# Bringing transposed activations through VectorE and DRAM instead of TensorE, in a fused attention and mixer block

## The chip, the cores and the metric

The kernel runs on one core of a Trainium2 chip. The metric is device time in microseconds (us), the median of several executions. Profiles are taken on one execution each; "span" is the time from its first to its last instruction, and the execution's own time is a little longer.

In the text TensorE, VectorE, ScalarE, GpSimd and SyncE are also called PE, DVE, ACT, POOL and SP, as in the profile. SP issues all DMAs of this kernel, in program order.

## The reference

With S = 2048 tokens of D = 576 features, all float32:

```python
x = A_x                       # (1, 2048, 576)
xn = _layernorm(x)
return x + _A_ref(xn, wqkv, wo) + _B_ref(xn, w1, w2, w3, w4)

# A: 32 heads of 18; token s attends to s, s-2, ..., s-14 (8 places); softmax; o @ wo
# B:
h  = gelu(layernorm(x) @ w1)                  # h in 4 channel groups
hs = concat(h[group g] shifted by +1,-1,+2,-2 tokens) @ w2
x1 = x + hs
return x1 + gelu(layernorm(x1) @ w3) @ w4     # hidden width 4608
```

Here the "x" of B is xn, the normalised input. Three tensors have to be turned from "token on a partition" to "feature on a partition" before a matmul can contract over features, besides xn itself: z = layernorm(xn), the layernorm of x1, and the attention output o.

## The kernel before

Tokens are handled in 16 tiles of 128 (index t), and in 4 blocks of 512 (index b). Y holds the running sum, token on partition, for all 16 tiles. Matmuls work on float32 split in two parts: a "hi" part rounded to fp32r and a "lo" part, the rest. A transposed block of 512 tokens is a tile of nine slices `[128, 9, 512]`: slices 0 to 3 the hi part of features 0 to 511, slice 4 the last 64 features (hi on partitions 0 to 63, lo on 64 to 127), slices 5 to 8 the lo part. A contraction over 576 features is 14 matmuls (the list PAIRS), whose first two read slice 0 and whose third reads slice 5.

Every engine executes its instructions in the order in which the program emits them (the schedule is manual); what looks concurrent is written out by hand, by placing each step at some iteration of a loop of matmuls. The stages:

1. **qkv.** For each tile t the x tile is loaded, normalised into Y, transposed (`prep_x`), and multiplied by wqkv in two halves (`q_half`); the result goes to DRAM (`qkvd`). Transposed blocks live in `ring`, a pool of two buffers, asked for with `ring_block(key)`.
2. **mix.** For each block b: four `mix_tile` and one `mix_rem`, in the order tiles 0, 1, 2, the remainder, tile 3. They multiply z by w1 (14 matmuls of 512 columns, or 9), and ScalarE applies gelu twice as it evicts PSUM, once to the hi part and once to float32; VectorE subtracts for lo. `mix_rem` also moves rows between partitions with eight small DMAs (v from u) and leaves five later steps in the list `todo`. w2 is loaded and split in this stage.
3. **W2 loop.** For each tile t: 28 matmuls of 288 columns (`mm_tok`), the result added to Y by VectorE, and the statistics of x1 (`stats`). Later the first weights of the MLP are split here too.
4. **MLP.** 72 units (c, b), c over pairs of 128 hidden channels, b over the token blocks. A unit runs two `up` (14 matmuls of 512 columns, two gelus, a subtraction) and the four `down` of the unit before (12 matmuls of 288 columns each, added to Y by VectorE). From the fourth unit on, `bg` interleaves pieces of the attention, which runs on VectorE from `qkvd`, head group by head group, and writes its output to `od` in DRAM; it ends before unit NU-4. The list LATE names the tiles of x1 that are normalised and transposed inside the first units; those of blocks 0 and 1 are handled within the W2 loop.
5. **Wo loop.** For each tile: o @ wo, with the load of o and of x, the sum and the store of the output.

PSUM has two buffers `psa` (tag a: mix_tile, mix_rem, up) and three `psb` (tag b: everything else). The transposition in use is `transposes`: four TensorE transposes of 128x128 per tile, one more for two tiles' tails of 64 features, then ScalarE copies PSUM to the hi slices and VectorE subtracts for the lo slices:

```python
for k in range(4):
    pe.transpose(p0[:, k, :], src[:, k * 128:(k + 1) * 128], ident)
if tail:
    pe.transpose(p1[:rows], tail[0], ident)
act.copy(xt[:, 0:4, c], p0)
dve.tensor_tensor(xt[:, 5:9, c], p0, xt[:, 0:4, c].bitcast(F32), op=ALU.subtract)
```

It is called by `prep_x` (x), `z_prep` (z, in the last four tiles of the qkv stage and in mix), `n_prep` (x1, tiles 6 to 13 of the W2 loop and units 0 to 5) and `prep_o` (o, in the final downs and the Wo loop). `z_norm` and `n_norm` write the normalised tile just ahead of it.

Of the kernel before, what the change touches and what calls it, by code (L numbers as in the profile page):

```python
# [45 lines left out]
def fused_block(ctx, tc, x, wqkv, wo, w1, w2, w3, w4, out):  # L46
# [19 lines left out]
    BN = base.tile([128, 4, 2, 6], F32, name="bn")  # L66
    qkvd = dram.tile([24, HALO + S, GC], F32, name="qkvd")
# [4 lines left out]
    def tail_half(t):  # L72
        if t % 2 == 0:
            ztail[t // 2] = base.tile([128, 128], F32, name="ztail", bufs=2)
        return ztail[t // 2][:, t % 2 * 64:t % 2 * 64 + 64]

    def norm_z(dst, kind, t):
        norm(dst, Y[:, t, :512], kind, t)
        norm(tail_half(t), Y[:, t, 512:], kind, t)
# [36 lines left out]

    def split_w(dst_hi, dst_lo, raw):
        act.copy(dst_hi, raw)  # L118
        dve.tensor_tensor(dst_lo, raw, dst_hi.bitcast(F32), op=ALU.subtract)
# [20 lines left out]
    zp = {}  # L140

    def z_norm(t):
        zp[t] = w1pool.tile([128, 512], F32, name="z", bufs=2)
        norm_z(zp[t], 1, t)

    def z_prep(t):
        xt = ring_block(("z", t // 4))
        transposes(zp[t], pair_tail(ztail[t // 2], xt, t), xt, (t % 4) * 128)
# [176 lines left out]
    load_w1(1)  # L325
    for t in range(4, NT):
        for h in range(2):
            q_half(t, h)
            if h == 0:
# [11 lines left out]
            else:  # L341
                if t == NT - 4:
                    z_norm(0)
                    z_norm(1)
                if NT - 3 <= t < NT - 1:
                    z_prep(2 * (t - NT + 3))
                    z_norm(2 * (t - NT + 3) + 2)
# [13 lines left out]
    pool.memset(T4[:, S:S + 4].bitcast(F32), 0.0)  # L361

    def load_w2(k):
        r = mpool.tile([128, D], F32, name="rz", tag="rz", bufs=2)
# [11 lines left out]
    def mix_tile(b, m):  # L376
# [5 lines left out]
        g32 = mpool.tile([128, 512], F32, name="g32", bufs=1)  # L382
        c = 2 + b * 512
        hi = H[0][m][:, c:c + 512]
        act.activation(hi, ps, AF.Gelu_apprx_tanh)
        act.activation(g32, ps, AF.Gelu_apprx_tanh)
# [4 lines left out]
    def mix_rem(b):  # L391
# [4 lines left out]
        u = mpool.tile([128, 512], F32, name="u", bufs=2)  # L396
        v = mpool.tile([128, 512], F32, name="v", bufs=2)
        act.copy(u, ps)
# [23 lines left out]
    for b in range(NB):  # L422
        for i, m in enumerate((0, 1, 2, 4, 3)):
            nz = 4 * (b + 1) + i
# [44 lines left out]
    def n_norm(t, zpool):  # L469
        zp[t] = zpool.tile([128, D], F32, name="rz", tag="rz", bufs=2)[:, :512]  # L470
        norm_z(zp[t], 2, t)

    def n_prep(t):
        xt = x1n.get(t // 4)
        if xt is None:
            xt = x1n[t // 4] = ring_block(("n", t // 4))
        transposes(zp[t], pair_tail(ztail[t // 2], xt, t), xt, (t % 4) * 128)
# [3 lines left out]
    for t in range(NT):  # L481
        ps = psb.tile([128, 2, 512], F32, name="ps", tag="b")
        if 6 <= t < 14:
            n_norm(t - 6, mpool)
# [17 lines left out]
        if 6 <= t < 14:  # L502
            n_prep(t - 6)
        if 2 <= t and todo:
            todo.pop(0)()
    mp.__exit__(None, None, None)
# [5 lines left out]
    hp = ctx.enter_context(tc.tile_pool(name="hp", bufs=2, reuse_waits="tile"))  # L512

# [98 lines left out]
    def up(c, b, i):  # L612
# [7 lines left out]
        act.activation(hi, ps, AF.Gelu_apprx_tanh)  # L620
        act.activation(g32, ps, AF.Gelu_apprx_tanh)  # L621
# [23 lines left out]
    LATE = {(0, 0): (8, 9), (0, 1): (10, 11), (1, 0): (12,), (1, 1): (13,), (2, 0): (14,), (2, 1): (15,)}  # L645
    Wo = None
    oT = {}
# [25 lines left out]
    otile, xagain = {}, {}  # L673

    def load_o(t):
        if t % 2 == 0 and t < NT:
            src = od[t * 128:(t + 2) * 128, :].rearrange("(a p) d -> p a d", a=2)
            otile[t // 2] = opool.tile([128, 2, 512], F32, name="ot", bufs=2)
            sp.dma_start(otile[t // 2], src[:, :, :512])
            ztail[t // 2] = base.tile([128, 128], F32, name="ztail", bufs=2)  # L680
            sp.dma_start(ztail[t // 2].rearrange("p (a c) -> p a c", a=2), src[:, :, 512:])
# [6 lines left out]
    def prep_o(t):  # L688
        if t >= NT:
            return  # L690
        oT[t] = opool.tile([128, 9, 128], F32R, name="oT", bufs=3)
        o = otile[t // 2]
        tail = (ztail[t // 2], [(oT[t - 1], 0), (oT[t], 0)]) if t % 2 else None
        transposes(o[:, t % 2, :], tail, oT[t], 0)
        dve.tensor_tensor(Y[:, t, :], Y[:, t, :], xagain[t], op=ALU.add)

    for u, (c, b) in enumerate(units):
# [5 lines left out]
        if u == NU - 4:  # L703
            while not state["done"]:
                bg(1e9)
            open_wo()
            load_wo(0)
            load_wo(2)
        if u == NU - 3:
            split_wo(0)  # L710
            load_wo(4)
            load_o(0)
            load_o(2)
# [6 lines left out]
        for i in range(C):  # L720
            bg(r, False)
            ts = LATE.get((u, i), ())
            for t in ts:
                n_norm(t, hp)
            up(c, b, i)
            for t in ts:
                n_prep(t)
# [68 lines left out]
```

## Time and profile before

| | |
|---|---|
| median of 3 runs | 1323.08 us (1322.8 to 1323.17) |
| profiled execution | 1322.94 us, span 1321.2 us |
| TensorE matmuls busy | 1312.1 us (99%) |
| VectorE busy | 921.9 us (70%) |
| ScalarE busy | 348.2 us (26%) |
| GpSimd busy | 35.2 us (3%) |
| DMA | 93.76 MB, mean 71 GB/s |

A row of a group reads: line, engine, operation, output <- inputs, shapes, count, then busy us, mean ns of one, and the idle time of the engine just before, with what ended it. "L102" is line 102 of the kernel before. Matmuls are pipelined, so the duration of one is longer than the distance to the next: what a piece of TensorE's stream costs is read from start to start. A row of the timeline gives start us, us, engine, line and operation, with equal neighbours merged. A row of the table by window gives the window, its length, each engine's busy time, the granted TensorE clock (1.00 is full), the busy share of the DMA engines and GB/s.

### The profile page before, as it was taken

How to read it: one execution, taken by the hardware profiler on the slowest of the kernel's cores; microseconds unless marked ns; L12 is line 12 of the kernel's file. 1: busy time of each engine (PE TensorE's matmuls, PEld its weight loads, DVE VectorE, ACT ScalarE, POOL GpSimd, SP SyncE). 2: the span in 40 equal slices, each digit the busy share in tenths (PEclk: the TensorE clock that was granted, in tenths of full speed). 3: DMA queues.
4: the chain of work that ended last, by engine and by line, in shares of the span. 5: the costliest groups of instructions: out<-in, count | busy, mean ns of one | idle time of the engine just before them, and what ended most of it. 6: DMA issues, size and time to landing. Idle time of an engine off the chain costs nothing.

```text
span 1321.2 us, 18855 instructions
## 1 busy us (share of the span) xinstructions
PE 1312.1 (99%) x7894; PEld 1208.0 (91%) x7894; DVE 921.9 (70%) x1332; ACT 348.2 (26%) x633; POOL 35.2 (3%) x92
## 2 busy tenths in 40 slices
PE   8999999999999999999999999999999999999998
PEld 8999998899899999999999999999999999999998
DVE  6443326687676778878868868878877886884454
ACT  4322225411423222222122222223213223122111
POOL 2010100011000000000000000000000000000000
PEclk9999999999999999999999999999999999999999
DMA  7644322020112021221221220220320200212164
GB/s 211 152 107 108 98 68 69 18 82 28 59 30 80 20 71 39 71 71 39 71 71 29 80 71 20 90 71 20 90 71 19 82 28 20 71 42 95 46 192 140
DMA packets 120325, 93.76 MB, mean 71 GB/s; under 512 B 73504, under 2 KB 100000, under 8 KB 120240
## 3 DMA queue, kind: packets, MB, share of 16 engines
q1 hardware_dynamic: 120240, 92.56, 23.9%
q8 instruction: 62, 1.02, 0.3%
q14 instruction: 23, 0.19, 0.0%
HBM read 67.83 MB, written 23.66 MB: 69 GB/s over the span
## 4 chain that ended last, share of the span: by engine, by line
PE 96%; DVE 2%; ACT 1%; SPq 1%; issue 1%; DMA 0%; POOL 0%; DVEq 0%; ACTq 0%; POOLq 0%
PE ps L636 34%; PE p L616 34%; PE ps L133 18%; PE ps L230 3%; PE p L380 3%; PE ps L102 2%; PE p L272 0%; PE p L395 0%; PE p L764 0%; DVE bn L88 0%; PE ps L105 0%; ACT xt L107 0%; DVE xt L111 0%; SPq L370 0%; DVE xt L114 0%
## 5 line engine op out<-in xcount | busy, mean ns | idle before, releaser
L636 PE MATMUL ps<-W,hi 128*128 128x288 f32 x2304 | 397.9, 294 | 0.5 <-DVE oT L114 0.5
L636 PEld LDWEIGHTS ps<-W,hi 128*128 128x128 f32 x2304 | 339.5, 188 | 6.1 <-PE ps L102 0.7
L620 ACT ACTIVATE hi<-p 128x512 fp32r<-128x512 f32 x144 | 86.2, 599 | 619.3 <-PE p L616 619.3
L636 PE MATMUL ps<-W,lo 128*128 128x288 f32 x1152 | 245.3, 294 | 0.0
L616 PE MATMUL p<-xt,W 128*128 128x512 f32 x1008 | 235.4, 390 | 0.0
L616 PE MATMUL p<-x1n,W 128*128 128x512 f32 x1008 | 234.9, 389 | 0.0
L622 DVE TENSOR_TENSOR lo<-g,hi 128x512 fp32r<-128x512 f32 x144 | 99.7, 692 | 193.2 <-ACT g L621 193.2
L639 DVE TENSOR_TENSOR Y<-ps,Y 128x576 f32<-128x576 f32 x288 | 212.8, 751 | 16.3 <-PE ps L636 16.1
L616 PEld LDWEIGHTS p<-x1n,W 128*128 128x128 f32 x1008 | 187.2, 188 | 36.8
L616 PEld LDWEIGHTS p<-xt,W 128*128 128x128 f32 x1008 | 187.1, 188 | 36.9
L636 PEld LDWEIGHTS ps<-W,lo 128*128 128x128 f32 x1152 | 185.4, 187 | 0.0
L133 PE MATMUL ps<-WQ,xt 128*128 128x432 f32 x672 | 135.3, 360 | 0.0
L133 PEld LDWEIGHTS ps<-WQ,xt 128*128 128x128 f32 x672 | 125.2, 188 | 5.2
L111 DVE TENSOR_TENSOR xt<-ps,xt 128x512 fp32r<-128x512 f32 x40 | 27.6, 689 | 87.2 <-ACT xt L110 52.1
L568 DVE TENSOR_TENSOR prod<-q,k 128x1152 f32<-128x1152 f32 x64 | 86.5, 1351 | 0.0
L571 DVE TENSOR_REDUCE L<-prod 128x64 f32<-128x1152 f32 x64 | 86.2, 1347 | 0.0
L621 ACT ACTIVATE g<-p 128x512 f32<-128x512 f32 x144 | 85.4, 593 | 0.0
L548 DVE TENSOR_TENSOR prod<-v,L 128x1152 f32<-128x1152 f32 x56 | 75.6, 1350 | 0.0
L552 DVE TENSOR_TENSOR o<-o,prod 128x1152 f32<-128x1152 f32 x56 | 75.6, 1350 | 0.0
L118 ACT CAST W<-rawf 128x640 fp32r<-128x640 f32 x72 | 50.5, 702 | 68.9 <-PE ps L636 62.2
L133 PE MATMUL ps<-Wo,oT 128*128 128x288 f32 x420 | 59.1, 298 | 0.2
L133 PEld LDWEIGHTS ps<-Wo,oT 128*128 128x128 f32 x420 | 56.2, 188 | 1.4 <-issue 1.4
(103 smaller groups left out, 941.9 us busy)
## 6 DMA issues: line engine op xcount, KB each, us to landing
qkvd<-stg SPq DMA_DIRECT2D x24, 432.0 KB, 3.4
rawf<-in_B_w_dram SPq DMA_DIRECT2D x36, 288.0 KB, 3.0
rawf<-in_B_w_dram SPq DMA_DIRECT2D x36, 256.0 KB, 2.9
xin<-in_A_x_dram SPq DMA_DIRECT2D x16, 288.0 KB, 3.8
q<-qkvd SPq DMA_DIRECT2D x8, 576.0 KB, 3.8
k<-qkvd SPq DMA_DIRECT2D x8, 576.0 KB, 5.7
v<-qkvd SPq DMA_DIRECT2D x8, 576.0 KB, 5.9
od<-o SPq DMA_DIRECT2D x8, 576.0 KB, 4.9
```

Source lines behind the costliest of these rows:

```text
L118: act.copy(dst_hi, raw)
L133: pe.matmul(ps[:, h, :n], xs(a), ws(b, h), start=i == 0, stop=i == len(PAIRS) - 1)
L548: dve.tensor_tensor(dst, vv, Lf[:, :, w:w + 1].to_broadcast([128, TPP * GH, HD]), op=ALU.mult)
L552: dve.tensor_tensor(o, o, dst, op=ALU.add)
L568: dve.tensor_tensor(prod.rearrange("p (j h) d -> p j (h d)", h=GH), q, k[:, r0:r0 + TPP, :], op=ALU.mult)
L571: dve.tensor_reduce(Lf[:, :, w], prod, axis=AX.X, op=ALU.add)
L616: pe.matmul(ps, W3[f][:, w, :], x1n[b][:, a, :], start=n == 0, stop=n == len(PAIRS) - 1)
L620: act.activation(hi, ps, AF.Gelu_apprx_tanh)
L621: act.activation(g32, ps, AF.Gelu_apprx_tanh)
L622: dve.tensor_tensor(lo, g32, hi.bitcast(F32), op=ALU.subtract)
L636: pe.matmul(ps[:, k, :HF], h[:, col], w[:, p, k * HF:(k + 1) * HF], start=n == 0, stop=n == len(seq) - 1)
L639: dve.tensor_tensor(yv, ps[:, :, :HF], yv, op=ALU.add)
```

## The change

TensorE no longer transposes z, x1 and o; it still transposes x. In place of that:

- `turn(src, t)`: VectorE transposes the 576 columns of a normalised tile in 32x32 squares, in two instructions, into the staging tile ST `[128, 20, 128]` (the tail twice). A 32x32 transpose stays within its quadrant of 32 partitions, so the feature blocks are still in the wrong partitions.
- `put(key)`: after four tiles, four DMAs write ST, 32 partitions each, to a DRAM buffer `[5, 128, 512]`, so that every feature finds its row. ST is a single buffer.
- `get(key, xt)`: one DMA reads the buffer back into slices 4 to 8 of the transposed block.
- `split_x(xt)`: for the whole block, three ScalarE copies make the hi slices and two VectorE subtractions the lo slices.

The columns of a block then stand in the order (quadrant, tile, token) and not (tile, quadrant, token). For z and x1, ScalarE puts them in order as it evicts (`in_order` reads PSUM permuted, `by_token` writes in token order). For o the load is permuted instead: `load_o` reads a block of o in four DMAs, one per quadrant.

The steps are placed anew. z: turns in tiles 7, 8, 10, 11, 13 and 14 of the qkv stage and in mix block 0; the read of block b+1 at the start of mix block b and its split after the third mix step. x1: turns of blocks 0 and 1 in tiles 4 to 7 and 9 to 12 of the W2 loop, reads in tiles 9 and 14, splits in tiles 11 and 15; block 2 in the two ups of unit 0, block 3 in unit 1; their reads and splits in units 1 and 2, between the ups. o: turns with the downs of the last three units and in tiles 0 to 3 of the Wo loop, reads and splits one unit later, for block 3 in tiles 5 and 7. The five steps that `mix_rem` leaves are all done by tile 3 of the W2 loop.

```diff
+    def turn(src, t):
+        c = slice(32 * t, 32 * t + 32)
+        dve.transpose(ST[:, 4:20, c], src[:, :512].rearrange("p (j c) -> p j c", c=32))
+        dve.transpose(ST[:, 0:4, c].rearrange("p (a j) c -> p a j c", a=2),
+                      src[:, 512:].rearrange("p (j c) -> p j c", c=32)[:, None, :, :]
+                      .to_broadcast([128, 2, 2, 32]))
+
+    def put(key):
+        xd[key] = dram.tile([5, 128, 512], F32, name="xd", bufs=4)
+        for q in range(4):
+            sp.dma_start(dram_ap(xd[key], 128 * q, [[512, 32], [32 * 512, 20], [1, 128]]),
+                         ST[32 * q:32 * q + 32])
+
+    def get(key, xt):
+        sp.dma_start(xt[:, 4:9, :].bitcast(F32), xd[key].rearrange("k p c -> p k c"))
+
+    def split_x(xt):
+        raw = xt.bitcast(F32)
+        act.copy(RT[64:128, :], raw[64:128, 4, :])
+        act.copy(xt[0:64, 4, :], raw[0:64, 4, :])
+        act.copy(xt[:, 0:4, :], raw[:, 5:9, :])
+        dve.tensor_tensor(xt[64:128, 4, :], raw[64:128, 4, :], RT[64:128, :].bitcast(F32),
+                          op=ALU.subtract)
+        dve.tensor_tensor(xt[:, 5:9, :], raw[:, 5:9, :], raw[:, 0:4, :], op=ALU.subtract)
+
+    def in_order(blk):
+        return blk.rearrange("p (q t c) -> p t q c", q=4, t=4)
+    def by_token(blk):
+        return blk.rearrange("p (t q c) -> p t q c", q=4, t=4)
+    def quads(t_, b, q):
+        return dram_ap(t_, (512 * b + 128 * q) * D, [[D, 32], [32 * D, 4], [1, D]])
...
+    ZT = {7: 0, 8: 2, 10: 4, 11: 6, 13: 8, 14: 10}
     for t in range(4, NT):
         for h in range(2):
             q_half(t, h)
...
-                if t >= NT - 2:
-                    z_prep(2 * (t - NT + 2) + 1)
-                    z_norm(2 * (t - NT + 2) + 3)
+                if t == 12:
+                    get(("z", 0), ring_block(("z", 0)))
+            elif t == 13:
+                split_x(xring["z", 0])
+            if t in ZT:
+                z_turn(ZT[t] + h)
+                if h and ZT[t] % 4 == 2:
+                    put(("z", ZT[t] // 4))
+    get(("z", 1), ring_block(("z", 1)))
...
-        act.activation(hi, ps, AF.Gelu_apprx_tanh)
-        act.activation(g32, ps, AF.Gelu_apprx_tanh)
+        act.activation(by_token(hi), in_order(ps), AF.Gelu_apprx_tanh)
+        act.activation(by_token(g32), in_order(ps), AF.Gelu_apprx_tanh)
...
     for b in range(NB):
+        if 0 < b < NB - 1:
+            get(("z", b + 1), ring_block(("z", b + 1)))
         for i, m in enumerate((0, 1, 2, 4, 3)):
...
-            if b + 1 < NB and i < 4:
-                z_prep(nz)
-                if nz + 2 < NT:
-                    z_norm(nz + 2)
+            if b + 1 < NB and i == 2:
+                split_x(xring["z", b + 1])
+            if b == 0 and i > 0:
+                z_turn(12 + i - 1)
+                if i == 4:
+                    put(("z", 3))
...
+    def n_turn(t, zpool):
+        z = zpool.tile([128, D], F32, name="rz", tag="rz")
+        norm(z, Y[:, t, :], 2, t)
+        turn(z, t % 4)
+        if t % 4 == 3:
+            put(("n", t // 4))
...
+        while len(todo) > max(0, 3 - t):
             todo.pop(0)()
...
+        k = {4: 0, 5: 1, 6: 2, 7: 3, 9: 4, 10: 5, 11: 6, 12: 7}.get(t)
+        if k is not None:
+            n_turn(k, rzpool)
+        if t in (9, 14):
+            nb = t // 14
+            x1n[nb] = ring_block(("n", nb))
+            get(("n", nb), x1n[nb])
+        if t in (11, 15):
+            split_x(x1n[t // 15])
...
-    LATE = {(0, 0): (8, 9), (0, 1): (10, 11), (1, 0): (12,), (1, 1): (13,), (2, 0): (14,), (2, 1): (15,)}
+    LATE = {(0, 0): (8, 9), (0, 1): (10, 11), (1, 1): (12,)}
...
+    def load_o(b):
+        if b < NB:
+            otile[b] = opool.tile([128, 4, D], F32, name="ot", bufs=1)
+            for q in range(4):
+                sp.dma_start(otile[b][32 * q:32 * q + 32], quads(od, b, q))
+    def o_turn(b, t):
+        turn(otile[b][:, t, :], t)
+        if t == 3:
+            put(("o", b))
...
             up(c, b, i)
-            for t in ts:
-                n_prep(t)
+            for t in LATE.get((u, i), ()):
+                n_turn(t, tp)
+            if u in (1, 2) and i == 0:
+                get(("n", u + 1), x1n[u + 1])
+            if u in (1, 2) and i == 1:
+                split_x(x1n[u + 1])
+            if u >= NU - 2 and i == 0:
+                get(("o", u - NU + 2), o_block(u - NU + 2))
...
             for j in range(4):
                 bg(r, j == 1)
                 down(*prev, j)
+                if u == 1 and j < 3:
+                    n_turn(13 + j, tp)
+                if u >= NU - 3:
+                    o_turn(u - NU + 3, j)
+                if u >= NU - 2 and j == 1:
+                    split_x(xo[u - NU + 2])
+            if u >= NU - 3:
+                load_o(u - NU + 4)
...
+    get(("o", 2), o_block(2))
     for j in range(4):
         if j < 3:
-            prep_o(j)
+            add_x(j)
             load_xa(j + 2)
         down(*prev, j)
+    split_x(xo[2])
...
     for t in range(NT):
+        if b == 0:
+            o_turn(3, s)
+        if t == 5:
+            get(("o", 3), o_block(3))
+        if t == 7:
+            split_x(xo[3])
```

More of the change, by code (lines that the diff above doesn't have):

```diff
@@ L139, in fused_block, with z_turn @@
     W1R = w1pool.tile([128, 5, 128], F32R, name="W1R")
[L140 to L148, printed above, removed]
+    room(w1pool)
+    def z_turn(t):
+        z = w1pool.tile([128, D], F32, name="z", bufs=1)
+        norm(z, Y[:, t, :], 1, t)
+        turn(z, t % 4)
     qp = tc.tile_pool(name="qp", bufs=1, reuse_waits="tile")
@@ L467, in fused_block @@
     x1n = {}
[L469 to L477, printed above, removed]
+    def n_turn(t, zpool):
+        z = zpool.tile([128, D], F32, name="rz", tag="rz")
+        norm(z, Y[:, t, :], 2, t)
+        turn(z, t % 4)
+        if t % 4 == 3:
+            put(("n", t // 4))
     load_f(0)
@@ L686, in load_xa, with o_block, add_x @@
             sp.dma_start(xagain[t], xf[t * 128:(t + 1) * 128, :])
[L688 to L695, printed above, removed]
+    def o_turn(b, t):
+        turn(otile[b][:, t, :], t)
+        if t == 3:
+            put(("o", b))
+    def o_block(b):
+        if b < 2:
+            xo[b] = ring_block(("o", b))
+        else:
+            xo[b] = xp.tile([128, 9, 512], F32R, name=f"x1n{b}")
+        return xo[b]
+    def add_x(t):
+        if t < NT:
+            dve.tensor_tensor(Y[:, t, :], Y[:, t, :], xagain[t], op=ALU.add)
     for u, (c, b) in enumerate(units):
```

78 lines of the change are left out of this document (34 added, 44 removed).

## The prediction

> **What bounds the kernel now.** I read the page first, then TensorE's instructions in order of time around the three places where z, x1 and o are transposed, then the merged chain of waits, the prices by tile, and the DMA rows.
>
> ```profile
> span 1321.2 us, 18855 instructions
> ...
> PE 1312.1 (99%) x7894; PEld 1208.0 (91%) x7894; DVE 921.9 (70%) x1332; ACT 348.2 (26%) x633; POOL 35.2 (3%) x92
> ...
> PE 96%; DVE 2%; ACT 1%; SPq 1%; issue 1%; DMA 0%; POOL 0%; DVEq 0%; ACTq 0%; POOLq 0%
> ```
>
> TensorE (PE) is the bound: every microsecond off its stream comes off the span, and every wait it is given is added, since there is hardly an idle moment to absorb one. The profiled execution took 1322.94 us, 0.14 us from the median of the runs (1323.08), so I add to and take from 1322.9.
>
> Start times in order, from three windows of TensorE's timeline, and the merged chain:
>
> ```profile
> 172.88 0.60 PE L102 MATMUL ps<-ident,z 128*128 128x128 f32 x4
> 173.23 5.77 PE L133 MATMUL ps<-WQ,xt 128*128 128x432 f32 x28
> ...
> 196.80 3.36 PE L380 MATMUL p<-xt,W 128*128 128x512 f32 x14
> ```
> ```profile
> 245.86 13.01 PE L380 MATMUL p<-xt,W 128*128 128x512 f32 x56 [0.39 <-ACT g L386]
> 258.70 2.20 PE L395 MATMUL p<-xt,W1R 128*128 128x512 f32 x9
> 260.74 3.34 PE L380 MATMUL p<-xt,W 128*128 128x512 f32 x14
> 263.92 3.34 PE L133 MATMUL ps<-W,h 128*128 128x288 f32 x24
> ...
> 267.62 3.35 PE L133 MATMUL ps<-W,h 128*128 128x288 f32 x24
> ```
> ```profile
> 365.36 6.35 PE p L616 x28
> ...
> 1216.44 6.36 PE p L616 x28
> 1229.14 6.36 PE p L616 x28
> ```
> ```profile
> 1314.04 3.87 PE L764 MATMUL p<-Wo,oT 128*128 128x288 f32 x28
> ```
>
> **What is removed.** Undisturbed pieces first. A mix block is four mix_tiles, 258.70 - 245.86 = 12.84, and one mix_rem, 260.74 - 258.70 = 2.04: 14.88. A token tile of the W2 loop (and of the Wo loop, also 28 matmuls of 288 columns) is 267.62 - 263.92 = 3.70. A unit of the MLP is 1229.14 - 1216.44 = 12.70, of which the two ups take 6.35 and the four downs the other 6.35. Against these:
>
> - z: the mix stage ran 263.92 - 196.80 = 67.12; four blocks are 59.52. Saved 7.6, and four tiles in the qkv stage at 173.23 - 172.88 = 0.35 give 1.4 more: 9.0.
> - x1: W2 loop and units 0 to 2 ran 365.36 - 263.92 = 101.44; 16 x 3.70 + 6.35 + 2 x 12.70 = 90.95 (unit 0 has no downs). Saved 10.5.
> - o: from the last unit to the last tile 1314.04 - 1229.14 = 84.90; 12.70 + 6.35 + 15 x 3.70 = 74.55. Saved 10.35.
>
> Together 29.9 us, small stalls included. If all else were hidden the time would be 1293.
>
> **What is added: prices.** Everything else must hide under TensorE. The rows nearest to the new operations:
>
> ```profile
> L119 DVE TENSOR_TENSOR WQ<-raw,WQ x13: 451/758/1509, 7.5 to 45.2; 128x288 fp32r<-128x288 f32 x5, 128x864 fp32r<-128x864 f32 x4, 128x576 fp32r<-128x576 f32 x2, 128x1296 fp32r<-128x1296 f32 x2
> ```
> ```profile
> L118 ACT CAST WQ<-raw x13: 427/680/1278, 6.7 to 44.2; 128x288 fp32r<-128x288 f32 x5, 128x864 fp32r<-128x864 f32 x4, 128x576 fp32r<-128x576 f32 x2, 128x1296 fp32r<-128x1296 f32 x2
> ```
> ```profile
> L94 DVE TENSOR_SCALAR z<-Y,mv,rs x16: 536/542/549, 160.0 to 242.0; 128x512 f32<-128x512 f32 x16
> ```
> ```profile
> 316.41 0.76 DVE L495 TENSOR_TENSOR Y<-ps,Y 128x576 f32<-128x576 f32 x1 [0.19 <-PE ps L133]
> ...
> 318.37 0.68 DVE L111 TENSOR_TENSOR xt<-ps,xt 128x512 fp32r<-128x512 f32 x1
> ```
> ```profile
> L620 ACT ACTIVATE hi<-p 128x512 fp32r<-128x512 f32 x144 | 86.2, 599 | 619.3 <-PE p L616 619.3
> ```
>
> The shortest and longest of L119 (288 and 1296 columns) give VectorE 1.05 ns a column, of L118 ScalarE 0.84. So split_x on 2048 columns is 1.51 + 752 x 0.00105 = 2.3 us on VectorE (plus 0.7 for the 512-column tail) and, on ScalarE, 1.28 + 752 x 0.00084 = 1.9 plus two copies of 0.6: 3.1. ScalarE goes first, so a block is ready 3.1 + 2.3 = 5.4 after its read has landed. No row shows a VectorE transpose. The fastest 512-column row is 0.54, the dearest case twice L119's rate, 1.2; I take 0.6 (one pass over the columns) and 0.27 for the 128-column one. A turn with its norm (about 0.58) is then 1.45 us, without it 0.87; an add of Y with its statistics is 318.37 - 316.41 = 1.96. A gelu that reads in permuted order costs 0.6 by L620; if it doubled, two would take 2.4, still under the 3.18 us of the 14 matmuls behind them, so I cost it at nothing.
>
> The DRAM trip has no row, but its parts do:
>
> ```profile
> 410.00:411.00 1.00, 1.00 (x10) 1.00 (x9) 0.00 (x0) 1.00 (x3) 0.00 (x0) 1.00 1.00 406
> 532.80:533.80 1.00, 1.00 (x6) 0.84 (x5) 0.56 (x1) 0.00 (x0) 0.00 (x0) 1.00 1.00 245
> ```
> ```profile
> q<-qkvd SPq DMA_DIRECT2D x8, 576.0 KB, 3.8
> ...
> od<-o SPq DMA_DIRECT2D x8, 576.0 KB, 4.9
> ```
>
> With every DMA engine busy, 288-byte rows written to DRAM go at 245 GB/s, long rows read at 406. Less its bytes, the od write leaves 4.9 - 0.59/0.245 = 2.5 us of fixed time, the q read 3.8 - 0.59/0.406 = 2.35. put moves 640 x 2 KB = 1.31 MB in 512-byte rows: 5.7 us at 406, 7.8 at 245; I take 7.0, nearer the short-row end. get moves the same in 2 KB rows: 5.5. A trip is 12.5 us (9.5 to 13.5), and 12.5 + 5.4 = 17.9 from the last turn to the block. [...]
>
> **x1, where it is late.** T counts from the start of the W2 loop (263.92). VectorE and ScalarE run in program order, so an early split_x holds all that follows it: the next adds of Y, which free psb, and the gelus, which free psa. Turns 0 to 3 end near T = 34.4 (tile 7's matmuls end at 29.6; the steps left from mix_rem and two weight splits put VectorE a microsecond or two behind). Block 0: put 41.4, read 46.9, ScalarE 50.0, VectorE 52.3; psb covers that. But tile 12's add now starts at 52.3, so turn 7 ends at 55.8. Block 1: put 62.8, read 68.3, ScalarE 71.4, VectorE 73.7. TensorE has done unit 0's ups at 59.2 + 6.35 = 65.6, and the next up needs block 1 and a psa buffer whose gelu stands behind the split: about 73. **7 us lost.**
>
> Block 2: after 73.7 VectorE does two lo and four turns (7.2): 80.9; put 87.9. Ahead of the read on SP stand the five loads of attention (576 KB three times, 504 KB twice: 2.8 MB, 9 us at some 300 GB/s), so read 99.8, ScalarE 102.9, VectorE 105.2, first add 105.9. TensorE ran two ups and the three downs that psb holds, to 84.1. **21.8 lost.** Block 3: three more turns and adds, 111.7; put 118.7, read 124.2, split 129.6, add 130.3; TensorE stands from 118.6: **11.7 lost.** Sum 40.5.
>
> **Mix.** M counts from 196.80. Block 1 is read at M = 7.2, but its split follows the third gelu (10.8): VectorE done 16.2, block due 14.9: 1.2 lost. Block 2's read comes on SP behind the load of W2 row 3, eight v moves, the put of z's block 3 and eight small W2 loads:
>
> ```profile
> 211.97 0.59 SPq L400 DMA_DIRECT2D v<-u  x1
> ...
> 216.40 0.59 SPq L401 DMA_DIRECT2D v<-u  x1
> 217.08 3.76 SPq L370 DMA_DIRECT2D rz<-in_B_w_dram  x8
> ```
>
> VectorE frees W2's buffer after split_x and a turn, M = 18.5 to 19; the v moves take 216.40 + 0.59 - 211.97 = 5.0: 24; the put's four issues 2.4; the small loads 3.8: 30.4. Read 35.9, ScalarE 39.0, VectorE 41.3, while block 2 is due at 16.1 + 14.9 = 31.0: 9.6 lost. Block 3: 0.8. Sum 11.6.
>
> **o.** The read of o for block 0 goes behind load_wo:
>
> ```profile
> 1205.23 0.38 SPq L663 DMA_DIRECT2D rawf<-in_A_wo_dram  x1
> ```
>
> It lands near 1212, and the turns end at 1218.2 with the downs of the third-last unit. From then on a block has this cycle: put 7.0; load_o's data behind the put's, landed at +10; turn, add, turn +12.5; get's data behind both, landed +13.2, split +18.6; two adds and two turns +21.8. A unit is 12.70, so VectorE ends at 1240.0 and 1261.8, the last down at 1264.9 instead of 1229.14 + 12.70 + 6.35 = 1248.2: 16.7 lost. Tile 1 of the Wo loop then waits for an add behind add_x(2), whose xagain load stands on SP behind get(o, 2): 8.3 more. Sum 25. The last block has time: read by about 1301, used at tile 12. The qkv stage has slack for its puts (a tile is two halves of 5.6 us).
>
> **Sum:** 1322.9 - 29.9 + 40.5 + 11.6 + 25.0 = 1370.
>
> **Rivals.**
>
> - All is covered, 1293, faster. It decides at the trip: seven trips lie on the path (three of x1, one of z, three of o), so each microsecond off one is worth 7. The 77 us of stalls sink below 29.9 when a trip is under 12.5 - 47.2/7 = 5.8 us. For: TensorE's stream does lose 29.9. Against: the two fixed times alone are 4.85. Chance 0.06.
> - Short trips: 512-byte rows move as fast as long ones and reads start at once, 9.5 us; 3 x 7 = 21 less: 1349. For: the fixed times come from loaded queues. Chance 0.24.
> - Only x1 is late; in mix and o a buffer or the queue order leaves more room than I found: 1322.9 - 29.9 + 40.5 = 1333.5. Chance 0.08.
> - Restarts run slow. TensorE starts the program slowly:
>
> ```profile
> L272 PE MATMUL p<-ident 128*128 128x128 f32 x24 | 5.4, 423 | 1.4 <-POOL ident masks.py:199 1.4
> ```
>
> These 24 take 5.4 us, later four take 0.35 (172.88 to 173.23), so 24 would take 2.1: 3.3 lost. If each long stall ends so, three are followed by work that sets the end (after z's block 2, x1's block 3, tile 1 of Wo): 10 us, 1380. No row shows it after a stall within the span, and the granted clock reads 1.00 in the windows, so the sum has it at nothing. [...] In the same case I count dearer additions: transposes at 1.2 us put some 0.6 on each of the 15 or so turns that stand on these chains, 9 us, together up to 1390. Chance 0.2.
>
> The forecast itself, 1355 to 1375, has 0.42.
>
> **How the numbers follow.** About 0.2% (2.6 us) is what a measurement can tell here. Only the first rival is faster: 0.06. Same would need stalls of 27 to 32 us, between the first and third: 0.02. Slower 0.92. The range leaves out the first rival, most of the third and the far end of the fourth: 1335 to 1392.
>
> **What would show it.** Right: TensorE's transposes fall from 290 to the 74 of x and its idle time rises from 9 us to some 80, named VectorE, ScalarE or a DMA, in three clusters: one stall near 10 us in mix, three behind the W2 loop of which the middle is the longest, two or three in the last 130 us. A single trip put to get near 12.5. Wrong: TensorE still 99% busy, trips near 6 us, or stalls within u >= 3, where I expect none from permuted gelus.

## The result

The changed kernel took 1412.91 us (median; 1411.92 to 1417.27), the kernel before 1322.97 us beside it: a ratio of 1.0686, interval 1.0664 to 1.0709. It is 89.9 us slower. The prediction said slower, 1370 us, at most 1392; the mechanism came true and the size did not.

The page of the changed kernel, its span, TensorE's row, the granted clock by slices, and the chain by engine:

```profile
span 1411.5 us, 18421 instructions
PE 1305.7 (93%) x7678; PEld 1198.5 (85%) x7678; DVE 942.9 (67%) x1324; ACT 347.6 (25%) x573; POOL 36.8 (3%) x92
PEclk9999998998679999999999999999999999998789
PE 75%; DMA 9%; DVE 6%; SPq 4%; ACT 3%; issue 1%; ACTq 0%; DVEq 0%
```

TensorE fell from 99% to 93% busy: 9 us of idle time became 106. 216 instructions fewer took only 6.4 us off its busy time, because some ran at a lower granted clock (mean 0.963, before 1.000), which the third line shows around slices 7, 11 and 38. On the chain, 22% of the span now belongs to DMAs, VectorE, SP and ScalarE (9, 6, 4 and 3%; 4% before).

TensorE's timeline, the first matmul of each stage and those that end a long stall (in brackets the idle time before, and what ended it):

```profile
194.68 9.70 PE L421 MATMUL p<-xt,W 128*128 128x512 f32 x42
...
240.53 1.22 PE L421 MATMUL p<-xt,W 128*128 128x512 f32 x2 [12.77 <-ACT u L439]
242.37 10.67 PE L421 MATMUL p<-xt,W 128*128 128x512 f32 x40 [0.62 <-DVE xt L146]
...
274.52 1.75 PE L173 MATMUL ps<-W,h 128*128 128x288 f32 x12
...
352.21 9.56 PE L670 MATMUL p<-xt,W 128*128 128x512 f32 x28 [11.19 <-ACT g L675]
387.67 1.33 PE L690 MATMUL ps<-W,hi 128*128 128x288 f32 x4 [21.14 <-DVE Y L693]
413.99 1.33 PE L690 MATMUL ps<-W,hi 128*128 128x288 f32 x4 [11.40 <-DVE Y L693]
417.04 7.60 PE L670 MATMUL p<-x1n,W 128*128 128x512 f32 x28
...
1282.75 6.52 PE L670 MATMUL p<-x1n,W 128*128 128x512 f32 x28
1319.25 1.30 PE L690 MATMUL ps<-W,hi 128*128 128x288 f32 x4 [12.64 <-DVE Y L693]
1350.11 28.16 PE L173 MATMUL ps<-Wo,xt 128*128 128x288 f32 x196 [12.92 <-DVE Y L693]
1404.44 3.87 PE L843 MATMUL p<-Wo,x1n 128*128 128x288 f32 x28
```

The stalls stand in three clusters, as forecast. The differences of these starts, set against those of before, give each stage's share:

| stage | before | after | forecast | measured |
|---|---|---|---|---|
| qkv, to mix | 196.80 | 194.68 | -1.4 | -2.1 |
| mix | 67.12 | 79.84 | +4.0 (-7.6 + 11.6) | +12.7 |
| W2 loop and units 0 to 2 | 101.44 | 142.52 | +30.0 (-10.5 + 40.5) | +41.1 |
| the middle | 863.78 | 865.71 | 0 | +1.9 |
| last unit to last tile | 84.90 | 121.69 | +14.65 (-10.35 + 25) | +36.8 |

The sum of the differences is +90.4. The trips that set these stalls, on SP (start, time on the queue, line; `xd<-st` is put, `xt<-xd` and `x1n<-xd` are get, `ot<-od` is load_o):

```profile
219.77 4.41 SPq L133 DMA_DIRECT2D xd<-st  x4
224.28 6.05 SPq L411 DMA_DIRECT2D rz<-in_B_w_dram  x8
230.43 0.39 SPq L137 DMA_DIRECT2D xt<-xd  x1
...
309.86 4.18 SPq L133 DMA_DIRECT2D xd<-st  x4
318.41 0.38 SPq L137 DMA_DIRECT2D xt<-xd  x1
...
1302.21 4.14 SPq L133 DMA_DIRECT2D xd<-st  x4
1306.46 4.41 SPq L732 DMA_DIRECT2D ot<-od  x4
1311.06 0.38 SPq L137 DMA_DIRECT2D xt<-xd  x1
1328.96 4.14 SPq L133 DMA_DIRECT2D xd<-st  x4
```

and on ScalarE, the first instruction of each split, which waits for the read:

```profile
236.94 0.61 ACT L141 CAST rt<-xt 64x512 fp32r<-64x512 f32 x1 [12.72 <-DMA xt<-xd]
324.54 0.62 ACT L141 CAST rt<-xt 64x512 fp32r<-64x512 f32 x1 [38.27 <-DMA xt<-xd]
1320.61 0.61 ACT L141 CAST rt<-xt 64x512 fp32r<-64x512 f32 x1 [21.18 <-DMA xt<-xd]
```

With nothing beside it a put takes 318.41 - 309.86 = 8.55 us and the read 324.54 - 318.41 = 6.1: a trip of 14.7, where the prediction had 7.0 + 5.5 = 12.5. The puts of blocks 1 and 3 of x1 took 8.4 and 8.6, their reads 6.4 and 6.1. In the o stage the same two take 8.85 and 9.55, since load_o stands between them on SP, with the DMA engines 84% and 89% busy in the two stretches (79% and 67% in those of block 0).

The prices of the added instructions, in groups by line (count, total, mean ns):

```profile
L125 DVE STREAM_TRANSPOSE st<-rz 128x512 f32<-128x512 f32 x16 | 11.4, 712 | 10.0 <-DMA xd<-st 9.5
L126 DVE STREAM_TRANSPOSE st<-rz 128x128 f32<-128x128 f32 x16 | 4.3, 270 | 0.0
L143 ACT CAST xt<-xt 128x2048 fp32r<-128x2048 f32 x8 | 15.2, 1898 | 0.0
L146 DVE TENSOR_TENSOR xt<-xt 128x2048 fp32r<-128x2048 f32 x8 | 18.3, 2293 | 13.0 <-ACT xt L143 13.0
L674 ACT ACTIVATE hi<-p 128x512 fp32r<-128x512 f32 x144 | 86.1, 598 | 605.6 <-PE p L670 605.6
```

These were right or near: 0.71 and 0.27 for a turn (forecast 0.6 and 0.27), 1.9 and 2.3 for the split as forecast, 598 ns for a gelu in permuted order against 599 in plain order.

### The profile page after: what moved, and what is told of

It reads as the page before. It is cut to its first block, busy times and chain, and to the rows that moved or that the text cites. A ratio compares the mean times of both kernels' runs of the same rounds, so it can differ in the third digit from the quotient of the medians.

```text
span 1411.5 us, 18421 instructions
## 1 busy us (share of the span) xinstructions
PE 1305.7 (93%) x7678; PEld 1198.5 (85%) x7678; DVE 942.9 (67%) x1324; ACT 347.6 (25%) x573; POOL 36.8 (3%) x92
## 2 busy tenths in 40 slices
DMA packets 157636, 125.20 MB, mean 89 GB/s; under 512 B 72416, under 2 KB 129632, under 8 KB 157552
## 4 chain that ended last, share of the span: by engine, by line
PE 75%; DMA 9%; DVE 6%; SPq 4%; ACT 3%; issue 1%; ACTq 0%; DVEq 0%
PE p L670 29%; PE ps L690 29%; PE ps L173 12%; DMA xt<-xd 3%; PE ps L267 3%; DMA x1n<-xd 2%; DMA xd<-st 2%; SPq L133 1%; DVE xt L146 1%; DVE st L125 1%; ACT xt L143 1%; PE p L421 1%; SPq L732 1%; DMA xa<-in_A_x_dram 1%; DVE Y L693 1%
## 5 line engine op out<-in xcount | busy, mean ns | idle before, releaser
L690 PE MATMUL ps<-W,hi 128*128 128x288 f32 x2304 | 404.4, 297 | 57.9 <-DVE Y L693 57.9
L690 PEld LDWEIGHTS ps<-W,hi 128*128 128x128 f32 x2304 | 345.1, 191 | 65.5 <-DVE Y L693 47.1
L690 PE MATMUL ps<-W,lo 128*128 128x288 f32 x1152 | 248.4, 297 | 0.0
L670 PE MATMUL p<-xt,W 128*128 128x512 f32 x1008 | 237.6, 392 | 11.3 <-ACT g L675 11.2
L670 PEld LDWEIGHTS p<-xt,W 128*128 128x128 f32 x1008 | 188.8, 189 | 49.8 <-ACT g L675 11.6
L693 DVE TENSOR_TENSOR Y<-ps,Y 128x576 f32<-128x576 f32 x288 | 212.1, 749 | 8.3 <-PE ps L690 8.3
L690 PEld LDWEIGHTS ps<-W,lo 128*128 128x128 f32 x1152 | 188.4, 190 | 0.0
L421 PE MATMUL p<-xt,W 128*128 128x512 f32 x224 | 55.4, 403 | 16.8 <-ACT u L439 13.4
L421 PEld LDWEIGHTS p<-xt,W 128*128 128x128 f32 x224 | 42.6, 193 | 29.0 <-ACT u L439 14.7
L159 DVE TENSOR_TENSOR W<-rawf,W 128x640 fp32r<-128x640 f32 x72 | 56.4, 785 | 0.0
```

Source lines behind the costliest of these rows:

```text
L421: pe.matmul(ps, W1[:, w, m * 128:(m + 1) * 128], xt[:, a, :], start=i == 0, stop=i == len(PAIRS) - 1)
L670: pe.matmul(ps, W3[f][:, w, :], x1n[b][:, a, :], start=n == 0, stop=n == len(PAIRS) - 1)
L690: pe.matmul(ps[:, k, :HF], h[:, col], w[:, p, k * HF:(k + 1) * HF], start=n == 0, stop=n == len(seq) - 1)
L693: dve.tensor_tensor(yv, ps[:, :, :HF], yv, op=ALU.add)
```

## The experiments

The theory (A) was: the block comes late by the length of its trip, VectorE and ScalarE are held by the split in their program order, and each stage pays for itself. Rivals: the parts share one cause (B), the added work costs wherever it stands (D), or another wait takes the place of any that is removed (E). C and F are rivals of single runs and are told there.

**One part at a time.** Each kernel keeps the new path for one tensor and gives the other two before's path back, with its loops (for x1, say):

```diff
+            n_norm(t - 6, rzpool)
...
+            n_prep(t - 6)
...
-            n_turn(k, rzpool)
```

> Only z goes through DRAM; x1 and o are transposed on TensorE as before. Theory A (each part pays for its own late trips, and the stall is local to its stage): the changed kernel's own stages give qkv -2.1 and mix +12.7, so 1322.9 + 10.6 = 1333.5, with the mix stage near 80 us and all later stages as before. Rival B (the parts share one cause, such as the slower clock or delays that are handed on from stage to stage): the mix stage alone does not reproduce 80 us, or later stages grow too. The terms of the prediction by themselves: -9.0 + 11.6 = +2.6, so 1325.5.

> Only x1 goes through DRAM; z and o are transposed on TensorE as before. Theory A: W2 loop and units 0 to 2 take 142.5 us as in the changed kernel (101.4 before), so 1322.9 + 41.1 = 1364.0 and nothing else moves. Rival B (handed on from mix): they take less than 142.5, and the three single changes add up to less than the 90 us of the whole. Terms of the prediction: -10.5 + 40.5 = +30, so 1353.

> Only o goes through DRAM; z and x1 are transposed on TensorE as before, the gelus evict in plain order. Theory A: from the last unit to the last tile 121.7 us as in the changed kernel (84.9 before), so 1322.9 + 36.8 = 1359.7. Rival B: clearly less, the rest being handed on from earlier stages. Terms of the prediction: -10.35 + 25 = +14.7, so 1337.6. If A holds, the three singles give 10.6 + 41.1 + 36.8 = 88.5 of the 90 us.

Measured 1334.2, 1366.05 and 1357.18, beside 1322.87 before: +11.3, +43.2 and +34.3, together 88.8 of 89.9. Each lies within 2.6 us of what A gave. Theory A holds: the three losses are separate, and no part is free.

**The shape of put's writes.** The writes of put, 128 partitions by five row blocks each:

```diff
-            sp.dma_start(dram_ap(xd[key], 128 * q, [[512, 32], [32 * 512, 20], [1, 128]]),
-                         ST[32 * q:32 * q + 32])
+            sp.dma_start(dram_ap(xd[key], 5 * 128 * 128 * q, [[128, 128], [128 * 128, 5], [1, 128]]),
+                         ST[:, 5 * q:5 * q + 5, :])
```

> The changed kernel, with each put issued as four writes of 128 partitions by five row blocks instead of four writes of 32 partitions by twenty; the bytes, the 512-byte rows and the number of writes stay. The rows land at other places of the DRAM block, so the numbers that are read back are in a wrong order; all work is otherwise the same. [...] Rival C (the 512-byte rows set the rate, whatever the partitions): put stays at 8.4 and the time within 3 us of 1412.9.

Measured 1394.57 us, 18.3 less, so rival C is out. SP in that kernel:

```profile
330.89 2.76 SPq L133 DMA_DIRECT2D xd<-st  x4
336.90 0.36 SPq L137 DMA_DIRECT2D xt<-xd  x1
```

This put (block 1 of x1) takes 6.0 us, 8.4 in the changed kernel; that of block 0 takes 7.4 instead of 8.55. The issues take 2.8 on SP instead of 4.1. 18.3 is seven to eight times the 2.4 saved. So the length of the trip is what the time hangs on, and it fell when each write covered 128 partitions instead of 32, at the same row length and with the same packets and bytes (157636 and 125.20 MB in both kernels). One thing more differs: these rows land back to back in DRAM, and not 2 KB apart. No run tells what part of the gain is due to that.

The next run asks whether each write is slow by itself, or only beside its neighbour:

```diff
-        for q in range(4):
+        for q in (0, 2, 1, 3):
             sp.dma_start(dram_ap(xd[key], 128 * q, [[512, 32], [32 * 512, 20], [1, 128]]),
...
-            for q in range(4):
+            for q in (0, 2, 1, 3):
                 sp.dma_start(otile[b][32 * q:32 * q + 32], quads(od, b, q))
```

> The changed kernel; the four writes of each put, and the four loads of a block of o, are issued in the order of quadrants 0, 2, 1, 3 instead of 0, 1, 2, 3. Nothing else changes. [...] Rival F (each 32-partition write is slow by itself, one after the other): within 3 us of 1412.9. [...]

Measured 1402.22 us, 10.7 less, by an exchange of order alone, with every row at its old place in DRAM. Put got shorter, by less than with 128 partitions:

```profile
332.71 3.91 SPq L133 DMA_DIRECT2D xd<-st  x4
340.18 0.38 SPq L137 DMA_DIRECT2D xt<-xd  x1
```

This put takes 7.5 us (7.8 for block 0), between the 6.0 (7.4) of writes of 128 partitions and the 8.4 (8.55) of the changed kernel. Rival F is out; what makes the order count was not shown. Each load of o went from 6.7 to 5.6 us to landing (median) and shares in the gain.

**The clock.** Windows of the changed kernel's first 4 us after two stalls, and the 4 us behind the first (length, busy time of PE and the others, then PEclk, DMA share, GB/s):

```profile
387.00:391.00 4.00, 3.33 (x13) 3.33 (x14) 3.93 (x8) 0.00 (x0) 0.00 (x0) 0.50 0.02 4
391.00:395.00 4.00, 4.00 (x17) 3.19 (x17) 3.51 (x7) 0.30 (x1) 0.00 (x0) 0.88 0.21 41
414.00:418.00 4.00, 4.00 (x15) 3.81 (x16) 1.99 (x4) 0.00 (x0) 0.00 (x0) 0.50 0.00 0
```

The granted clock is 0.50 after the stall: the down that starts at 387.67 takes 3.0 us instead of 1.6. In the next runs dummy transposes of the identity fill the stalls; fill(n, ...) issues n of them. One of the places:

```diff
+                if u in (1, 2) and j == 3:
+                    fill(225 if u == 1 else 110, psa, "a")
...
                 down(*prev, j)
```

> The changed kernel, with dummy transposes of the identity put into TensorE's stream ahead of the nine matmuls that wait longest, to fill most of each stall, so that no idle window precedes a restart; all else stays. In the changed kernel TensorE is busy 1305.7 us where 1312.1 less the busy time removed (29.9 less the 8 us of small stalls) would be about 1290: some 16 us are matmuls at half clock. Theory A (every slow restart is paid): 16 us go, 1397. Theory B (a slow restart followed by another stall, which VectorE or a transfer ends, is absorbed; only those of mix, of x1's block 3 and of tile 1 of Wo are paid, 2 to 3 us each): 5 to 9 us go, 1404 to 1408. Rival C (the halved clock only shows beside the stalls and costs nothing, or the idle windows are not its cause): within 3 us of 1412.9, or the clock still drops.

Measured 1415.37 us, with a mean clock of 0.996 instead of 0.963. A dummy took 0.110 us and one fill waited 9.5 us itself, so it was run again with fewer:

> The keep-warm kernel again with fewer dummies: one dummy measured 0.110 us (120 took 13.26) instead of the 0.0875 counted on, so that most fills outlasted their stall, and one fill in the last unit itself waited 9.5 us for its buffer; that one is left out, the others are cut to fit. In the first keep-warm kernel the last unit began 3.9 us earlier than in the changed kernel, and the last 15 tiles of Wo took 1.5 us less. Theory B (most slow restarts are absorbed by the next stall): 4 to 8 us go, 1405 to 1409. Theory A (all are paid): 1397. Rival C: within 3 us of 1412.9.

Measured 1412.29 us at a mean clock of 0.993: rival C by its number, 0.6 us from the changed kernel. But the trace shows where the gain went:

```profile
1346.16 26.18 PE L179 MATMUL ps<-Wo,xt 128*128 128x288 f32 x196 [1.55 <-DVE Y L701]
1372.18 7.57 PE L179 MATMUL ps<-Wo,x1n 128*128 128x288 f32 x56
1383.06 20.31 PE L179 MATMUL ps<-Wo,x1n 128*128 128x288 f32 x140 [3.31 <-DVE Y L855]
```

Tile 1 of Wo starts 3.9 us earlier (1346.16, not 1350.11), its first seven tiles take 2.0 us less, and then TensorE meets a new wait of 3.3 us for the last block, whose trip had been hidden, with a slow restart of its own behind it (20.15 us to the last tile, where five undisturbed tiles are 18.5). So 5.9 us were won by then, 3.3 of them already at the start of the last unit (1279.44 instead of 1282.75), and the last tile starts only 1.2 us earlier (1403.21 instead of 1404.44). Within x1's stage nothing was won at all (142.51 us instead of 142.52). The slow clock is real, and removing it was worth 0.6 us at the end: of the 5.9 us won on the way, later waits for VectorE or a transfer absorbed most. The fills are not free either (one of them still waited 3.2 us for its buffer), so that 0.6 is the balance of both.

**The same work earlier.** If lateness is the cause, the operations must be cheap where they are early.

```diff
-    ZT = {7: 0, 8: 2, 10: 4, 11: 6, 13: 8, 14: 10}
+    ZT = {4: 0, 5: 2, 7: 4, 8: 6, 10: 8, 11: 10, 13: 12, 14: 14}
...
-            if b + 1 < NB and i == 2:
+            if b + 1 < NB and i == 1:
                 split_x(xring["z", b + 1])
```

> Only z goes through DRAM, as in the z-only kernel (1334.2), but all sixteen turns lie in the qkv stage, so that the last block is written before mix begins, the reads in mix stand behind fewer entries of SP's queue, the split comes one tile earlier and the split of W2 row 2 moves to block 1. Theory A (only the late block costs): 9.0 us of transposes are gone and the 12 us stall with them, 1314 to 1317. Rival D (the added work of VectorE and ScalarE costs wherever it stands): the qkv stage or mix grows and the time stays at or above 1322.

Measured 1337.71 us, 3.5 more than z alone in its first order: a miss. TensorE lost 2.3, 7.8 and 10.0 us to gelus that stood behind a split. The early put did not help, since the read stood elsewhere on SP:

```profile
215.78 0.59 SPq L447 DMA_DIRECT2D v<-u  x1
216.41 0.59 SPq L448 DMA_DIRECT2D v<-u  x1
217.10 0.53 SPq L143 DMA_DIRECT2D xt<-xd  x1
```

Eight moves of v, themselves held by W2's loads until 211.99, go ahead of it; TensorE left the buffer at about 212.1, with the last tile of block 0, so that the read went 5 us late. The order was changed (`moves` holds the moves of v, which now go behind the read of the next block):

```diff
+        if b:
+            moves[b - 1]()
...
-            k = {(0, 1): 0, (0, 2): 1, (1, 2): 2, (1, 4): 3, (2, 4): 4}.get((b, i))
-            if k is not None:
+            for k in {(0, 0): (0, 1), (1, 2): (2,), (1, 4): (3,), (2, 4): (4,)}.get((b, i), ()):
```

> The early-z kernel (1337.7) stood 2.3, 7.8 and 10.0 us at the three block ends of mix, because each read was issued on SP behind W2 loads that waited for VectorE and behind eight moves of v. Here the same operations are put in another order: the read of the next block goes ahead of the moves, W2 rows 0 and 1 are split after the first tile so that the next loads do not hold SP, and the first step on u comes one tile later than the split. Theory A (order of SP's queue and of ScalarE's stream is what was late): 20 us of stalls fall to 0 to 3, 1314 to 1317. Rival D (the read and the split of a block, about 12 us, do not fit beside a block of 14.9 us of mix): stalls of 5 us or more stay, 1320 or above.

Measured 1327.03 us (ratio 1.0035, 1.0024 to 1.0045): 10.7 less, mix 71.95 us instead of 83.18, and still not below before. The time misses A's range by 10 us; by its number this is D. Stalls of 2.5, 1.5 and 3.0 us are left of 20, the first and the last with slow restarts (nine matmuls in 3.89 us instead of 2.20, and 56 in 15.70 instead of 13.01). Only the last stands behind a read and a split, as D says: read issued at 235.20, landed at 242.05, gelu behind the split at 245.0. The first ends with a gelu behind the splits of W2's rows, whose load landed at 204.76, the second with a copy behind the gelus on u. So 13 of the 20 us of stalls came from the order of SP's queue and of ScalarE's stream; what would be left with the first two mended was not run.

For o the attention is paced faster, so that the turns can start earlier:

```diff
-    RATE = [5.9, 5.9, 5.9, 5.9]
+    RATE = [6.3] * 4
...
-                if u >= NU - 3:
-                    o_turn(u - NU + 3, j)
+                if u in (NU - 8, NU - 6, NU - 4, NU - 2):
+                    o_turn((u - NU + 8) // 2, j)
```

> Only o goes through DRAM, as in the o-only kernel (1357.2), but attention is paced 7% faster so that it ends about five units earlier, one block is turned and written in every second unit from the eighth-last on, and each read goes as soon as its buffer is free, a unit ahead of its use. The operations on o are the same in number and size. Theory A (the trip is hidden when it is early): 1322.9 - 10.35 = 1312.5, up to 1316. Rival D (turns and splits cost on a VectorE that is over 80% busy there): stalls appear in the last ten units, and the time stays above 1322.

Measured 1333.83 us, 23.4 less than o alone at first and still D by its number, with 14.6 us of stalls left; block 0 was read only at 1220.7, behind Wo's loads, a put and a load. One unit earlier still (pace 6.4), with each read where its buffer falls free:

```diff
-            load_wo(2)
         if u == NU - 3:
+            load_wo(2)
...
+            if u >= NU - 4 and i == 1:
+                get(("o", u - NU + 4), o_block(u - NU + 4))
```

> The early-o kernel (1333.8) read block 0 only at 1220.7, behind Wo's loads, a put and the load of the last o block on SP, and two reads then shared the DMA engines. Here the turns come one unit earlier still (attention paced 8% faster than at first), Wo's loads one unit later, and each read is issued right after the second up of the unit that last uses its buffer. Theory A: no stall over 1 us is left in the last ten units, 1312.5 to 1316. Rival D (splits and turns on VectorE hold the adds wherever they stand): 1320 or above.

Measured 1316.84 us (ratio 0.9954, 0.9939 to 0.9969): 0.5% faster than before, 0.8 us above the range, one stall of 2.65 us being left. With the order of quadrants 0, 2, 1, 3:

> The kernel with the requeued o (1316.8), with the same order 0, 2, 1, 3 in put and in the loads of o. There the trips are hidden but for one wait of 2.65 us on VectorE. [...] Rival F: 1316.8 within 1 us.

Measured 1313.49 us, ratio 0.9928 (0.9912 to 0.9945), 3.35 us less than in the order 0, 1, 2, 3, so that rival F is out here too. TensorE in that kernel:

```profile
PE 1302.1 (99%) x7822; PEld 1198.7 (91%) x7822; DVE 930.1 (71%) x1340; ACT 347.3 (26%) x613; POOL 35.1 (3%) x92
```
```profile
1229.30 6.52 PE L670 MATMUL p<-x1n,W 128*128 128x512 f32 x28
1244.32 0.80 PE L690 MATMUL ps<-W,hi 128*128 128x288 f32 x4 [0.57 <-DVE Y L693]
1304.71 3.88 PE L834 MATMUL p<-Wo,x1n 128*128 128x288 f32 x28
```

From the last unit to the last tile it takes 75.4 us, against 84.9 before and 74.55 worked out for no stall at all; 9.3 us of the forecast 10.35 are won. The gain lies in this stage: from unit 3 to the last unit, where the attention is paced faster, the kernel takes 864.4 us, 863.8 before. This is the best version found.

**All three early.** 

> z and o as in the two early kernels; of x1 the tiles 0 to 7 go through DRAM with their turns three tiles earlier in the W2 loop, the tiles 8 to 15 are transposed on TensorE as before. Theory A: -9.0 - 10.35 and half of x1's 10.5: 1322.9 - 24.6 = 1298.3, with small stalls up to 1304. Rival D: at or above 1322.

Measured 1356.93 us. In this kernel the gelus of blocks 2 and 3 evict in permuted order though their tokens stand in plain order, so that tokens are mixed there. The stalls of the two early kernels came back (19.6 us in mix, 17 in the last units), and one of 7.8 us was new, since the norm of tile 8 stood behind the split of block 1. The second try:

> Both new orders together, and of x1 the tiles 0 to 7 through DRAM with early turns, block 1 split behind the first two norms of unit 0, tiles 8 to 15 on TensorE with their gelus in plain order. Theory A: -9.0 - 10.35 and half of x1's 10.5: 1298 to 1304. Rival D: 1316 or above, the parts being in each other's way.

Measured 1322.65 us (ratio 0.9998, 0.9984 to 1.0011): no difference, a miss by 19 us. Its ten runs spread from 1319.3 to 1326.5, and the profiled one, 1325.88, is near the slow end. There mix takes 73.1 us against 67.1 before, the W2 loop with units 0 to 2 102.8 against 101.4, and last unit to last tile 81.1 against 84.9. So half of x1 on the new path gains nothing: TensorE waits 3.85 us for the norms of tiles 10 and 11, which stand behind the split of block 1 on VectorE, and restarts slowly (the next up takes 4.95 us, the one ahead of the wait 3.46). In these runs only o pays, and by itself.

**Two terms by themselves.** Block loads of o in 128-partition rows:

```diff
-            for q in range(4):
-                sp.dma_start(otile[b][32 * q:32 * q + 32], quads(od, b, q))
+            for t in range(4):
+                sp.dma_start(otile[b][:, t, :], od[(4 * b + t) * 128:(4 * b + t + 1) * 128, :])
```

> The o-only kernel (1357.2), with each block of o loaded by four reads of 128 partitions, one token tile each, instead of four reads of 32 partitions; the bytes are the same, the tokens of a block lie in another order, so that the output's tokens are mixed. Theory A (a 32-partition transfer is slow, and the read of the block before queues behind it on the DMA engines, 9.6 us instead of 6.2): the four issues on SP take 2 instead of 4.4 us, the read 6.5 to 8, and with a first block and two cycles on the path some 6 to 12 us go: 1345 to 1351. Rival E (the load is hidden beside the put and the read; the cycle is set by put, split and turns): within 2 us of 1357.2.

Measured 1353.92 us, 3.3 less: between the two. The reads after the loads took 9.0, 7.9 and 8.2 us instead of 9.1, 9.8 and 9.2; the issues on SP did not shorten. Part of the cycle, not most of it.

Attention's first loads behind x1's read of block 2 (`if u == 2` instead of `if u == 1`):

> The x1-only kernel (1366.05), with attention begun at unit 2 instead of unit 1, so that its five first loads stand on SP behind the read of x1's block 2 and not ahead of it. Theory A: that read takes 6.3 instead of 10.9 us, block 2 and with it block 3 end 4 to 5 us earlier, 1361 to 1362. Rival E (another wait takes its place, for one the loads now ahead of the read of block 3): within 1.5 us of 1366.

Measured 1366.4 us, unchanged: E, as named. TensorE's stalls that end with the splits of block 2 and of block 3, in the x1-only kernel and then in this one:

```profile
377.94 1.33 PE L697 MATMUL ps<-W,hi 128*128 128x288 f32 x4 [20.78 <-DVE Y L700]
404.31 1.33 PE L697 MATMUL ps<-W,hi 128*128 128x288 f32 x4 [11.18 <-DVE Y L700]
```
```profile
372.35 1.33 PE L697 MATMUL ps<-W,hi 128*128 128x288 f32 x4 [15.64 <-DVE Y L700]
404.45 1.33 PE L697 MATMUL ps<-W,hi 128*128 128x288 f32 x4 [17.71 <-DVE Y L700]
```

Block 2 came 5.6 us earlier, its read taking 6.6 instead of 10.7 us; the loads then went ahead of the read of block 3, which ended where it had.

## Why the prediction was right, and where it was wrong

**Right.** TensorE as the bound and the 29.9 us that the change removes from it (9.3 of o's 10.35 were won once its trips were hidden). The prices of split and permuted gelu, and nearly that of a turn. That the trip decides, that VectorE and ScalarE are held by an early split, and the three clusters. That the middle stall is x1's longest was forecast too; its length, 21.14 us against 21.8, is in part luck, since both its ends came 7 to 8 us later than forecast.

**Wrong by 43 us.** The stages miss by 8.7 (mix), 11.1 (x1) and 22.1 (o), and the middle by 1.9; qkv came 0.7 better. The step that failed is the price of the trip, above all of put, and with it two smaller terms:

- *The trip.* Put was set at 7.0, between two rates of rows, as if its rows alone were its limit; it took 8.4 to 8.6, and less when each write covered 128 partitions or when the order of the four changed. With get at 6.1 instead of 5.5 a trip is 2.2 longer. The working for x1 has four trips in series, though the count of seven has three of them. TensorE goes on after block 3 at T = 139.5 (413.99) instead of 130.3. That is 9.2 of the 11.1 missing there; the down behind it at half clock (3.0 us instead of 1.6) makes another 1.4. The ups behind that, 7.4 us from start to start instead of 6.4, are 1.1 of the middle's 1.9.
- *What stands beside and ahead of a read.* In mix, put held SP for 4.41 us (2.4 forecast) and the eight small loads 6.05 (3.8), so that block 2's read went at M = 35.75, not 30.4, and landed at 42.3, not 35.9: 6.4 of the 8.7. (The working gives 41.3 - 31.0 = 10.3 us lost there, and not 9.6.) Slow matmuls behind the stall make 1.3 more (10.67 us for 40 instead of 9.37). In o the cycle was 26.8 us instead of 21.8: from put to read 1.9 more, the read 9.55 instead of the 6.2 left for it behind load_o, splits and turns 0.25 less. Two cycles make 10 of the 22 missing in o; the first put came 3.5 later against the last unit than forecast, tile 1 waited 12.9 instead of 8.3, and the seven tiles from it on took 2.1 more at a lower clock.
- *Slow restarts* were counted at nothing in the sum and at 10 us in a rival. The clock did drop to 0.50, but filling the stalls gave back 0.6 us at the end and at most 5.9 on the way: the rival's premise was right and its price too high. The slow start of the program, from which the rival was worked out, is no proof of it: the granted clock reads 1.00 there (0 to 8 us of the kernel before).

Put at 8.5, as it was measured, with the sevenfold weight, would have made it 1370 + 10.5 = 1380.5, still 32 us too low; the rest is the reads and issues beside other transfers, the fourth trip of x1 and the slow matmuls. The upper end of the range, 1392, came from the rival on restarts and from turns at 1.2 us, which took 0.71.

## What to carry to other kernels

Price a transfer by its shape and order, not only by its row length: with 512-byte rows each time, a put took 8.4 to 8.6 us in writes of 32 partitions, 7.5 to 7.8 in another order of them, and 6.0 to 7.4 in writes of 128 (rows back to back in DRAM). Take the time of its issues on the queue from a place where transfers are as dense (4.1 to 4.4 us here, 2.4 forecast). A trip through DRAM in several steps cost under 1 us where it was units ahead of its use (o in the best version, 75.4 us against 74.55), and its full length, times the number of trips in series, where it was not (18.3 us for 2.4 off a put); what has to move is the read's place in the queue, not only the write. Of a stall that can be shortened, ask which link is late next: here two repairs of 5 to 6 us (the filled stalls, and x1's read ahead of the loads) moved the end by less than one.

## What the runs showed of the hardware that was not expected

- Four writes of 32 partitions and 320 KB each took 8.4 to 8.6 us in the order 0, 1, 2, 3, 7.5 to 7.8 in the order 0, 2, 1, 3, and as writes of 128 partitions 6.0 and 7.4 us, with 512-byte rows each time (two puts of x1 in each kernel, and a third in the first).
- The issues of one put held SP for 4.1 us, 3.9 in the order 0, 2, 1, 3 and 2.8 with 128 partitions. The loads of o did not follow: with 128 partitions their issues still took 4.4. What sets the time on the issuing queue stays open.
- Idle times of 2.5 to 3.0 us were enough for a slow restart. In the kernel with the requeued z nine matmuls took 3.89 us after 2.53 idle, 2.20 undisturbed, and 56 took 15.70 after 3.05 idle, 13.01 after 0.17:

```profile
207.17 3.89 PE L442 MATMUL p<-xt,W1R 128*128 128x512 f32 x9 [2.53 <-ACT g L433]
211.22 13.01 PE L427 MATMUL p<-xt,W 128*128 128x512 f32 x56 [0.17 <-ACT g L433]
224.07 2.20 PE L442 MATMUL p<-xt,W1R 128*128 128x512 f32 x9
...
246.13 15.70 PE L427 MATMUL p<-xt,W 128*128 128x512 f32 x56 [3.05 <-ACT g L433]
```
